# One core: y and the next chunk's scores in one visit to the quarters of TensorE, and another order at the start

## The chip, the cores and the metric

The kernel runs on one core of a Trainium2 chip, and on nothing else: there is no second core to wait for. The metric is the device time of one execution in microseconds (us), and for several runs its median. A core has five engines that run their own instruction streams and wait for each other by semaphores: PE (TensorE, the matmuls), DVE (VectorE), ACT (ScalarE), POOL (GpSimd) and SP (SyncE, which here only starts DMAs). ACT can start DMAs too.

## The reference, cut to what matters

```python
# gla: batch 4, 8 heads, 768 positions, head size 48
for t in range(S):
    state = alpha[:, :, t, :, None] * state + einsum('bhd,bhe->bhde', k[:, :, t], v[:, :, t])
    y[:, :, t] = einsum('bhd,bhde->bhe', q[:, :, t], state)
# bridge: (B, H, S, D) -> (B*S, H*D), so x is 3072 x 384
h = x @ w_in          # 384 x 2048
g = h - tanh(h)
out = g @ w_out       # 2048 x 384
```

Inputs and output are float32 here but for the weights, which come in 64-bit form and are brought to float32 on the chip.

## The kernel before, in words

Units. The 3072 rows are cut into 12 units of 256 positions (`NU`), and each unit into two chunks of 128 (`CU`). Three units make one batch element. For each unit there is a recurrent part, `gla`, and a feed-forward part, `moe`. In what follows "u.c" is chunk c of unit u, and "u:s" is step s of unit u's feed-forward part, of which there are eight (`FS`).

The recurrent part. The decays are transposed (`aT`), two scans on DVE make running products backwards and forwards (`U`, L711, and `W`, L730), and k and q are scaled by them (`kU`, `qW`). Then TensorE works per chunk in two small pieces. `scores` (L782 to L812) multiplies k by q within half chunks and makes the updates of the state. `y` (`halves_products`, L864 to L890) multiplies q with the state and the masked scores with v. From unit 1 on both use the array as four quarters of 64 x 64: 32 matmuls each, which the trace holds as 64 records, since each of them is recorded twice. Between them DVE masks the scores (`masked`), adds up `mid` and `state`, and decays the state (`decay`). After y, ACT copies the features to `xT` (`features`, task "x") and DVE adds the rest (`rest`); SP then moves a few rows (`moves`). `back` and `natural` transpose k for a unit and copy it. Unit 0 is done in another way (`direct`), with full masks and full-width scores.

The feed-forward part. Step u:s has a first product on TensorE (`first`, L1075: 6 matmuls of 256 columns, 12 records), a square and a quadratic on ACT (`u`, `z`), a cube on DVE (`w`, which reads h in PSUM), the shrunk value `g`, from unit 2 on three sums `e`, and a second product (`second`, L1117: 7 matmuls of 192 columns and 14 records, in units 0 and 1 four of 384). The weights of units 0 and 1 arrive in 16 pieces that SP fetches (`load_weight`, L39; eight DMAs for a piece of w_in), ACT reads (L86, L87) and DVE converts (L89, L90).

PSUM. Its pools are `ps_sc` (one tile of two banks, "sc"), `ps_h` (two tiles of one bank, "h": the results of first products) and `ps_o` (one bank each for "o0" to "o3": the results of second products). In the kernel before, y, the scores and `back` of units 2 to 11 all use the two banks of "sc", one after another.

The order. Nothing is scheduled at run time. Every task is added to `Planner` with an engine, a length in us, a rank and the tasks that it follows. `order` (L387) lays the tasks out eight times, with priorities from the round before (from the fifth on with random changes), and keeps the layout that ends first; each engine gets its instructions in that order. A task that follows another one is held back by that one's latency `lat`, also where both are on one engine. `filler` (L1204 to L1210) puts dummy matmuls ("spin") where the plan leaves TensorE idle before y 0.0. The task `see` loads the word `ok`, which says whether the fast path was valid, into all engines; the last unit's `store` comes after it.

In the middle of the run TensorE goes first product, scores, second product, first product, y, second product for a chunk, then some pairs of first and second product without a visit, then the next chunk; once a unit `back` comes in between.

Of the kernel before, what the change touches and what calls it, by code (L numbers as in the profile page):

```python
# [38 lines left out]
def load_weight(nc, pool, rows, **kw):  # L39

    raw = pool.tile([P, WN], I64 if rows[0][2].dtype != FP32 else FP32, name="raw", **kw)
    for at, js, src in rows:
        nc.sync.dma_start(out=raw[at].rearrange("p (j n) -> p j n", n=src.shape[-1])[:, js], in_=src)
    return raw
# [277 lines left out]
class Planner:  # L322
# [64 lines left out]
    def order(self):  # L387
# [3 lines left out]
        for i, t in enumerate(self.tasks):  # L391
            edges = {names[a]: self.tasks[names[a]][6] for a in t[4]}
            if t[7]:
                edges.setdefault(names[t[7]], 0.0 if self.tasks[names[t[7]]][1] == t[1] else 0.25)
            for j, lat in edges.items():
                before[i].append((j, lat))
                after[j].append((i, lat))
# [17 lines left out]
        for x in plan:  # L415
            name, e, length = self.tasks[x[3]][:3]
            if e == engine and until:
                filled += [(free, -1, do, None)] * int(max(0.0, x[0] - free) / us)
# [6 lines left out]
def fast(tc, q, k, v, alpha, moe_w_in, moe_w_out, out, w_in, w_out, ident, ok, pad_rows):  # L425
# [17 lines left out]
    with ExitStack() as ctx:  # L443
# [90 lines left out]

        plan = Planner()
# [15 lines left out]
        def fetch(what, s):  # L551
            raw_of[what, s] = load_weight(nc, raw_pool, weight_parts(moe_w_in, moe_w_out, pad_rows, what, s), bufs=4)
# [10 lines left out]
        for n, (what, s) in enumerate(pieces):  # L563
            rank = RANK[what] + 2 * s
            held = pieces[n - 4] if n >= 4 else None
            add(f"fetch {what}{s}", "SP", 5.7 if n < 2 else 4.3 if what == "in" else 2.0, rank - 30, [held and f"read {held[0]}{held[1]}"],
# [36 lines left out]
        def gla(u, rank):  # L603
# [8 lines left out]
            parts = [(x, slice(c * NP, (c + 1) * NP), slice(c, c + 1)) for c, x in enumerate("ab")] if parted else [("", slice(0, N), slice(0, CU))]  # L612
# [3 lines left out]
            def go(name, engine, us, k, after, do, of=u, **kw):  # L616
                add(f"{name} {of}", engine, us, rank + k,
                    [a if a[-1] in "0123456789" else f"{a} {of}" for a in after if a], do, **kw)

            prev = f" {u - 1}" if u > 0 else None  # L620
            for what, name in enumerate(("aT", "kT", "qT", "v")):
# [5 lines left out]
                   lambda what=what: load(u, what), lat=2.9 if u == 0 else 3.6 if u < PLAIN else 4.5)  # L627

            def widen(what):
                for hh in range(2):  # L630
                    t, r0 = raws[what], HP * hh
                    to, of = t[r0 + 32:r0 + HP, :, :, 0:D - 32], t[r0:r0 + 32, :, :, 32:D]
                    A.copy(to, of)  # L633

            def flip(what, make):
                t = make()
                for g in range(NP):
                    to = t[:, g].rearrange("p c (i r) -> p r c i", r=R)
                    V.transpose(to, raws[what][:, g, :, 0:32])  # L639
# [42 lines left out]
            for n, ab in enumerate("ab"):  # L682
# [3 lines left out]
                if by_matmul(u, 1):  # L686
                    go(f"turn kT{ab}", "PE", 0.92, 1 + n * 0.1,
                       ["load kT"] + [later and x for x in ("x 0.0", "y 0.1", "state 0.1")], lambda n=n: turn(1, n))
                    for x, _, cs in parts:
                        go(f"kU{ab}{x}", "DVE", 0.33 if x else 0.6, 3, [f"turn kT{ab}", f"U{x}", n and f"kUa{x}", later and "back 0.1", later and by_matmul(u, 2) and "turn qTb"],  # L690
                           lambda n=n, cs=cs: times(1, "U", n, cs))
                if by_matmul(u, 2):
                    go(f"turn qT{ab}", "PE", 0.92, 2 + n * 0.1,
                       ["load qT", later and f"aT{ab}" if by_matmul(u, 0) else "masked 0.0"], lambda n=n: turn(2, n))
                    for x, _, cs in parts:
                        go(f"qW{ab}{x}", "DVE", 0.33 if x else 0.6, 5, [f"turn qT{ab}", f"W{x}", n and f"qWa{x}", later and "y 0.1", later and by_matmul(u, 1) and "turn kTb"],
                           lambda n=n, cs=cs: times(2, "W", n, cs))
            for what, (name, k_) in enumerate((("aT", 0), ("kT", 2), ("qT", 4))):
                if by_matmul(u, what):
                    continue  # L700
                go(f"wide {name}", "ACT", 1.3, k_ - 0.5, [f"load {name}"], lambda what=what: widen(what))
                go(name, "DVE", 1.9, k_, [f"wide {name}"] + ([f"y {u - 2}.{CU - 1}"] if u > 1 else []),
                   lambda what=what: flip(what, makes[what]))
# [43 lines left out]
            for x, ns, _ in parts:  # L747
                go(f"U{x}", "DVE", 1.13 if x else 2.2, 1, (["aTa", "aTb"] if by_matmul(u, 0) else ["aT"])
                   + (kU(u - 1) + [f"sizeU{prev}", f"least{prev}"] if prev else []), lambda ns=ns: scan_U(ns))
                go(f"ends{x}", "DVE", 0.3, 3, [f"U{x}"], lambda ns=ns: ends(ns))  # L750
                go(f"W{x}", "DVE", 1.13 if x else 2.2, 3, [f"ends{x}"] + (qW(u - 1) + [f"sizeW{prev}"] if prev else []),
                   lambda ns=ns: scan_W(ns))
            whole = [x for x, _, _ in parts]
            go("least", "DVE", 0.07, 7, [f"U{x}" for x in whole], shortest)
            if not by_matmul(u, 1):
                go("kU", "DVE", 1.12, 3, ["kT", "U"], lambda: scale("kT", "U"))
            if not by_matmul(u, 2):
                go("qW", "DVE", 1.12, 5, ["qT", "W"], lambda: scale("qT", "W"))
# [11 lines left out]
            def chunk(c):  # L770
# [11 lines left out]
                def scores():  # L782
                    if c == 0:

                        xT[u] = two.tile([P, NP, TU], FP32, name="xT")
                    if u == 0 and c == 1:
                        sc = m["sc", c] = [ps_h.tile([P, 2, TU], FP32, name="h").rearrange(
                            "p a t -> p (a t)").rearrange("p (g t) -> p g t", t=P) for _ in range(2)]
# [25 lines left out]
                def masked():  # L814
                    sc = m["sc", c]
                    if direct:
                        m["pm", c] = [two.tile([P, NP, P], FP32, name=f"pm{r}", tag=tag) for r, tag in enumerate("zw")]
                        for r, to in enumerate(m["pm", c]):
                            V.tensor_mul(to, sc[r] if c else sc[:, r], mask.unsqueeze(1).to_broadcast([P, NP, P]))
# [14 lines left out]

                def products():

                    if n == 0:
# [26 lines left out]
                def halves_products():  # L864
# [4 lines left out]
                    m["y", c] = banks((2, 3))  # L869
# [22 lines left out]
                def rest():  # L892

                    for hh in range(2):
                        rows = quads[hh]
                        if u >= PLAIN:
# [10 lines left out]
                def features():  # L907
# [5 lines left out]
                    if u >= PLAIN:  # L913
# [46 lines left out]
                else:  # L960

                    held = [f"masked {past}"] if u == 1 and c == 0 else [f"masked {past}", f"mid {past}", f"state {past}"] if u == 1 else [
                        f"x {past}", f"rest {past}"] if c else []
                    go_c("scores", "PE", 1.27, 7, kU(u, c) + qW(u, c) + [f"natural {u}", f"load v {u}"] + held, scores)
# [357 lines left out]
```

## Time and profile before

| what | value |
|---|---|
| median of 3 runs (lowest, highest) | 576.52 us (575.82, 578.79) |
| the profiled execution's own time | 578.48 us |
| its span, from the first to the last instruction | 576.7 us |
| mean clock granted to TensorE | 0.992 |
| DMA moved | 50.84 MB |

The profile is of one execution, slower than the median by 2.0 us. Sums made from the trace belong to its own time. Its columns and views are explained where they are shown. What matters in reading it: the page gives busy shares over the whole span; the chain of work that ended last says on which engine a saved microsecond counts; the timeline gives the start of each group of instructions, and differences of starts are firmer than the lengths of matmuls, whose ends are modelled. These are the costliest groups of the page on TensorE, with the count and the mean length in nanoseconds:

```profile
L1080 PE MATMUL h<-xT,w_in 128*128 128x256 f32 x1152 | 265.1, 380 | 0.6 <-DVE w_in L90 0.6
...
L1146 PE MATMUL o<-b,e 128*128 128x192 f32 x480 | 90.9, 326 | 0.0
```

The last columns are the idle time of the engine just before the group and what ended it.

### The profile page before, as it was taken

The page shows a single profiled execution, that of the slowest core. Times are in us where ns is not written, and L with a number is a line of the kernel's source. Part 1 is how long each engine was busy: PE and PEld are TensorE (multiplying, and loading weights), DVE is VectorE, ACT ScalarE, POOL GpSimd, SP SyncE. Part 2 cuts the span into 40 slices and gives each one's busy share as a digit, 9 for nine tenths or more (in the row PEclk, how much of TensorE's full clock was granted, in tenths as well). Part 3 has the DMA queues.
Part 4 walks back from the last instruction along what each step waited for, and adds up shares of the span by engine and source line. Part 5 has one row for each costly group of instructions (what it writes and reads, how often), then busy time and mean ns, then how long its engine had stood idle before and what let it go on. Part 6 is the DMA issues. An engine that isn't in the chain of part 4 may idle for free.

```text
span 576.7 us, 13746 instructions
## 1 busy us (share of the span) xinstructions
PE 565.9 (98%) x5583; PEld 500.1 (87%) x5583; DVE 450.8 (78%) x886; ACT 323.2 (56%) x559; POOL 4.8 (1%) x22
## 2 busy tenths in 40 slices
PE   8899999999999999999999999999999999999995
PEld 8787777778989999998999999898998999899995
DVE  5889879999999995895895896896797645554643
ACT  2589885747777686577485365364443433333530
POOL 3000000000000000000000000000000000000000
PEclk9799999999999999999999999999999999999999
DMA  8988781235674762562640320310200000000001
GB/s 181 211 220 243 233 182 56 85 70 137 113 155 120 121 161 84 118 158 71 185 116 1 85 61 3 75 51 22 53 12 1 30 7 3 28 8 0 28 1 35
DMA packets 60713, 50.84 MB, mean 88 GB/s; under 512 B 35776, under 2 KB 50400, under 8 KB 60640
## 3 DMA queue, kind: packets, MB, share of 16 engines
q1 hardware_dynamic: 57728, 48.88, 34.7%
q10 hardware_dynamic: 2912, 0.98, 0.8%
q8 instruction: 46, 0.75, 0.6%
q14 instruction: 27, 0.22, 0.1%
HBM read 44.04 MB, written 4.72 MB: 85 GB/s over the span
## 4 chain that ended last, share of the span: by engine, by line
PE 96%; DVE 2%; issue 1%; POOL 0%; ACT 0%; DVEq 0%; POOLq 0%
PE h L1080 43%; PE o L1146 32%; PE o L1125 7%; PE sc L805 2%; PE sc L878 2%; PE sc L888 2%; PE sc L811 2%; PE sc L991 1%; PE spin L1208 1%; PE turned L663 1%; DVE W L730 0%; PE sc L795 0%; PE h L795 0%; DVE w_in L90 0%; PE y L853 0%
## 5 line engine op out<-in xcount | busy, mean ns | idle before, releaser
L1080 PE MATMUL h<-xT,w_in 128*128 128x256 f32 x1152 | 265.1, 380 | 0.6 <-DVE w_in L90 0.6
L1080 PEld LDWEIGHTS h<-xT,w_in 128*128 128x128 f32 x1152 | 215.4, 190 | 28.0 <-DVE w_in L90 0.7
L1089 ACT ACTIVATE u<-h 128x512 f32<-128x512 f32 x96 | 57.0, 594 | 180.7 <-PE h L1080 180.2
L1097 DVE TENSOR_TENSOR w<-h,u 128x512 f32<-128x512 f32 x96 | 65.8, 686 | 79.1 <-ACT u L1089 78.7
L1146 PE MATMUL o<-b,e 128*128 128x192 f32 x480 | 90.9, 326 | 0.0
L1146 PE MATMUL o<-w_out,e 128*128 128x192 f32 x320 | 81.5, 337 | 0.0
L1146 PEld LDWEIGHTS o<-b,e 128*128 128x128 f32 x480 | 80.2, 190 | 0.0
L1101 DVE SCALAR_TENSOR_TENSOR g<-z,w 128x512 f32<-128x512 f32 x96 | 65.3, 682 | 4.1 <-PE o L1125 1.3
L1146 PE MATMUL o<-b,g 128*128 128x192 f32 x320 | 65.1, 326 | 0.0
L1093 ACT ACTIVATE z<-u 128x512 f32<-128x512 f32 x96 | 60.4, 629 | 2.6
L1146 PEld LDWEIGHTS o<-w_out,e 128*128 128x128 f32 x320 | 55.7, 189 | 4.4
L1146 PEld LDWEIGHTS o<-b,g 128*128 128x128 f32 x320 | 54.2, 190 | 0.0
L1107 ACT ACTIVATE big<-u 128x1024 f32<-128x1024 f32 x48 | 50.4, 1049 | 0.0
L1125 PE MATMUL o<-w_out,g 128*128 128x384 f32 x128 | 44.0, 488 | 0.0
L1125 PEld LDWEIGHTS o<-w_out,g 128*128 128x128 f32 x128 | 24.1, 190 | 13.7
L1113 DVE TENSOR_TENSOR e<-g 128x256 f32<-128x256 f32 x80 | 33.4, 418 | 1.8
L1114 DVE TENSOR_TENSOR e<-g 128x256 f32<-128x256 f32 x80 | 33.3, 416 | 0.0
L639 DVE STREAM_TRANSPOSE aT<-ar 128x256 f32<-128x256 f32 x44 | 28.4, 645 | 2.8 <-ACT ar L633 1.7
L730 DVE TENSOR_TENSOR_SCAN W<-aT,before 128x1032 f32<-128x1032 f32 (+1 forms) x13 | 27.7, 2132 | 0.0
L711 DVE TENSOR_TENSOR_SCAN U<-aT,after 128x1032 f32<-128x1032 f32 (+1 forms) x13 | 27.6, 2129 | 0.1
L1115 DVE TENSOR_TENSOR e<-g 128x128 f32<-128x128 f32 x80 | 22.6, 283 | 0.0
L639 DVE STREAM_TRANSPOSE qT<-qr 128x256 f32<-128x256 f32 x40 | 20.5, 629 | 0.0
(141 smaller groups left out, 560.3 us busy)
## 6 DMA issues: line engine op xcount, KB each, us to landing
raw<-in_moe_w_out_dram SPq DMA_DIRECT2D x16, 768.0 KB, 4.8
raw<-in_moe_w_in_dram SPq DMA_DIRECT2D x80, 96.0 KB, 4.0
raw<-in_moe_w_in_dram SPq DMA_DIRECT2D x16, 288.0 KB, 5.1
vt<-in_v_dram SPq DMA_DIRECT2D x23, 192.0 KB, 4.1
ar<-in_alpha_dram SPq DMA_DIRECT2D x44, 96.0 KB, 2.5
kr<-in_k_dram SPq DMA_DIRECT2D x40, 96.0 KB, 3.3
qr<-in_q_dram SPq DMA_DIRECT2D x40, 96.0 KB, 2.3
out_dram<-cross SPq DMA_DIRECT2D x19, 96.0 KB, 1.7
```

The source lines that it names most:

```text
L639: V.transpose(to, raws[what][:, g, :, 0:32])
L730: V.tensor_tensor_scan(out=m["W"][:, ns].rearrange("p n t -> p (n t)"), data0=aT[:, a:z], data1=before[:, a:z], initial=0.0, op0=ALU.mult, ...
L1080: T.matmul(h[:, a, :], lhsT=w_in[:, j, f * P:(f + 1) * P], rhs=xT[u][:, j, :], start=(j == 0), stop=(j == KT - 1))
L1089: A.activation(m["u", s], m["h", s], AF.Square, scale=W_SCALE ** -1.5)
L1093: A.activation(m["z", s], m["u", s], AF.Square, bias=QB, scale=QA * W_SCALE)
L1097: V.tensor_mul(m["w", s], m["h", s], m["u", s])
L1101: V.scalar_tensor_tensor(out=g.rearrange("p a c t -> p (a c t)"), in0=m["z", s], scalar=QK, in1=m["w", s], op0=ALU.add, op1=ALU.mult)
L1107: A.activation(big, m["us", s // 2].rearrange("p s t -> p (s t)"), AF.Relu, bias=-U_FAST, scale=W_SCALE, accum_out=over[:, n:n + 1])
L1113: V.tensor_add(e[:, 0:2, :], g[:, 0], g[:, 1])
L1114: V.tensor_sub(e[:, 2:4, :], g[:, :, 1, :], g[:, :, 0, :])
L1125: T.matmul(m["o"][c], lhsT=g[:, a, c, :], rhs=w_out[:, f, :], start=(f == 0), stop=(f == FT - 1))
L1146: T.matmul(o[n][:, i], lhsT=g_, rhs=w_, start=(s_ == 0 and (n, i) in ((0, 0), (1, 0), (2, 1), (3, 0))), stop=(s_ == FS - 1), skip_group_ch ...
```

## The change

- **Joint visits.** From unit 3 on (`JOINT`), y of a chunk is followed on TensorE at once by the scores of the next chunk. The place is fixed: `behind` names the step of the unit before after whose first product the pair comes (0 for chunk 0 and 4 for chunk 1, in unit 3 the steps 2 and 5), and `row`, a chain of tasks written out by hand, fixes the order of first products, second products and pairs from unit 2 on. After a pair come the second product of the step before and then two first products in a row.
- **y in other banks.** For these units y takes both tiles of "h" in place of the tile "sc". So y follows the cube of the last first product, and the next first product follows x and rest. As the tiles are now two, x is two copies and rest four adds, as in units 0 to 2 before.
- **Unit 0's scores** take banks of "o" and "h" in place of "sc", and `xT` is made with y.
- **Smaller tasks.** `widen` and `flip` are cut into pieces, and the scans U and W of every unit into two halves, each with its own `ends`.
- **The planner.** A task that follows one on the same engine (but for SP) is no longer held back by a latency. The rounds, the seed and the random changes are not touched by the diff. The dummy matmuls are counted with 0.24 us in place of 0.35 and in another formula. Lengths of tasks are changed, and ACT begins at 5.4.
- **The first piece of w_in** is fetched by ACT and SP in turn, four DMAs each; ACT's come after its copy of aT.

The built order of the changed kernel also differs where no line asks for it: the verdict's transpose comes after the last second product on TensorE, and unit 0's four products of k come before the first scan W on DVE.

```diff
-def load_weight(nc, pool, rows, **kw):
+def load_weight(nc, pool, rows, queues=None, **kw):
-    for at, js, src in rows:
-        nc.sync.dma_start(out=raw[at]..., in_=src)
+    for n, (at, js, src) in enumerate(rows):
+        (queues[n % len(queues)] if queues else nc.sync).dma_start(out=raw[at]..., in_=src)
...
-            edges = {names[a]: self.tasks[names[a]][6] for a in t[4]}
+            edges = {names[a]: 0.0 if self.tasks[names[a]][1] == t[1] != "SP" else self.tasks[names[a]][6] for a in t[4]}
...
-                filled += [(free, -1, do, None)] * int(max(0.0, x[0] - free) / us)
+                gap = x[0] - free
+                filled += [(free, -1, do, None)] * int(gap / (1.5 * us) if free == self.begin.get(engine) else (gap + 0.3) / us if gap > 0.2 else 0)
...
+        JOINT = PLAIN + 1
+        def behind(u, c):
+            return ((5 if c else 2) if u == JOINT else 4 * c) if u >= JOINT else None
+        def following(u, c):
+            after = (u, c + 1) if c + 1 < CU else (u + 1, 0)
+            return after if u >= JOINT and after[0] < NU else None
...
+                    if u == 0:
+                        sc = m["sc", c] = [(ps_h if c else ps_o).tile([P, NP, P], FP32, name="scores", tag="h" if c else f"o{r}")
+                                           for r in range(2)]
...
-                    m["y", c] = banks((2, 3))
+                    m["y", c] = banks((2, 3)) if u < JOINT else [ps_h.tile([P, NP, P], FP32, name="y", tag="h") for _ in range(2)]
...
+                near = [f"cube {u - 1}:{behind(u, c)}"] if behind(u, c) is not None else []
+                go_c("y", "PE", 1.19 if following(u, c) else 1.29, 9, near + ["masked", "mid", ...], halves_products)
...
+        joint = {(u - 1) * FS + behind(u, c): [f"y {u}.{c}"] + [f"scores {v}.{c_}" for v, c_ in [following(u, c) or (NU, 0)] if v < NU] for u in range(JOINT, NU) for c in range(CU)}
+        for at in range(PLAIN * FS, NU * FS + 2):
+            first, second, third = (f"{n // FS}:{n % FS}" for n in (at, at - 2, at - 1))
+            row += [f"first {first}"] * (at < NU * FS)
+            if at in joint:
+                row += [f"second {second}"] + joint[at] + [f"second {third}"]
+            elif at - 1 not in joint:
+                row.append(f"second {second}")
...
                 add(f"first {me}", "PE", 2.59, r, [...]
+                    + [f"{what} {u + 1}.{c}" for c in range(CU) if u + 1 < NU and behind(u + 1, c) == s - 1 for what in ("x", "rest")], first)
...
-        plan.filler = "PE", "y 0.0", 0.35, spin
-        plan.begin.update(SP=0.8, PE=1.5, ACT=3.0, DVE=4.8)
+        plan.filler = "PE", "y 0.0", 0.24, spin
+        plan.begin.update(SP=0.8, PE=1.5, ACT=5.4, DVE=4.8)
```

## The prediction

> **What bounds the kernel now.** I read the page's busy table, its forty slices and the chain that ended last first: is one engine the bound from end to end, and where is it not?
>
> ```profile
> span 576.7 us, 13746 instructions
> ...
> PE 565.9 (98%) x5583; PEld 500.1 (87%) x5583; DVE 450.8 (78%) x886; ACT 323.2 (56%) x559; POOL 4.8 (1%) x22
> ...
> PEclk9799999999999999999999999999999999999999
> ...
> PE 96%; DVE 2%; issue 1%; POOL 0%; ACT 0%; DVEq 0%; POOLq 0%
> ```
>
> TensorE carries 96% of the chain. So a microsecond taken out of TensorE's own sequence is worth a microsecond, and DVE and ACT count only where they make it wait. Two places are not covered by that: the second slice, where the clock digit is 7, and the last slice, where TensorE's digit is 5. I then opened the timeline of TensorE in the steady part, at one first product with a second product behind it, and at the two kinds of visit to the quarters.
>
> ```profile
> 208.60 2.77 PE L1080 MATMUL h<-xT,w_in 128*128 128x256 f32 x12
> 211.30 0.69 PE L805 MATMUL sc<-qT,kT 48*64 48x64 f32 x32
> 211.81 0.62 PE L811 MATMUL sc<-vt,kn 64*64 64x48 f32 x32
> 212.36 0.59 PE L1146 MATMUL o<-w_out,e 128*128 128x192 f32 x2
> ...
> 214.74 2.75 PE L1080 MATMUL h<-xT,w_in 128*128 128x256 f32 x12
> 217.42 0.34 PE L878 MATMUL sc<-qT,state 48*64 48x64 f32 x8
> 217.59 0.30 PE L878 MATMUL sc<-qT,mid 48*64 48x64 f32 x8
> ...
> 217.94 0.65 PE L888 MATMUL sc<-pm,vt 64*64 64x64 f32 x32
> 218.51 0.59 PE L1146 MATMUL o<-w_out,e 128*128 128x192 f32 x2
> ...
> 220.90 2.75 PE L1080 MATMUL h<-xT,w_in 128*128 128x256 f32 x12
> 223.49 0.49 PE L1146 MATMUL o<-w_out,e 128*128 128x192 f32 x2
> ...
> 225.76 2.75 PE L1080 MATMUL h<-xT,w_in 128*128 128x256 f32 x12
> ```
>
> Columns are start, length, engine, line. The reader is to take differences of starts. A first and a second product without a visit take 225.76 - 220.90 = 4.86 us. With the y visit the same pair takes 220.90 - 214.74 = 6.16, with the scores visit 214.74 - 208.60 = 6.14. A visit costs 1.30 or 1.28 us.
>
> How much of it is work? Inside y the third and fourth groups of 8 records start 0.12 apart (the chain gives the last 31 records 0.47), so about 14.7 ns a record: 64 records are 0.94. The scores have 32 such records (0.47) and 32 of L811 at 0.44 in the chain: 0.91. So 1.30 - 0.94 = 0.36 and 1.28 - 0.91 = 0.37 us of each visit is going in and coming out: about 0.15 before and in the first group (217.42 comes 2.68 after the first product's start where 2.59 is usual, and the first group takes 0.17, not 0.12), the rest in the second product after it (2.39 rather than 2.27, and a late start).
>
> The start and the end, by windows and the timeline:
>
> ```profile
> 15.00:20.00 5.00, 3.00 (x24) 2.58 (x23) 2.88 (x9) 2.45 (x5) 0.00 (x0) 0.75 0.77 197
> 20.00:25.00 5.00, 5.00 (x54) 4.12 (x54) 4.75 (x9) 2.82 (x5) 0.00 (x0) 0.57 1.17 256
> ```
>
> After the window and its length stand busy time and count of PE, PEld, DVE, ACT, POOL, then the clock. TensorE idles 2 us before 17.64 (the waits put it on DVE's qT) and then runs at half clock until about 24.3: the same 16 score records take 2.08 us here.
>
> ```profile
> 565.25 0.27 PE L1239 MATMUL sc<-ident,fine 128*1 128x128 f32 x1
> ...
> 565.57 0.28 DVE L1243 TENSOR_REDUCE ok<-sc 1x1 int32<-1x128 f32 x1 [0.21 <-PE sc L1239]
> ...
> 568.17 0.49 ACT L1184 ACTIVATE p<-o 128x384 f32<-128x384 f32 x1 [4.96 <-PE o L1146]
> ```
>
> The verdict's transpose stands in front of TensorE's last 28 records; the queues load ok at 565.9 (0.47 us), and p starts before TensorE has ended.
>
> **What the Trainium skill says.** TensorEngine Tiling (Array Packing), Tiling Modes: changing the tiling mode drains the engine, moving to another tile in the same mode doesn't. The trace agrees: 0.36 us at the borders of a visit, none seen between L805 and L811 or L878 and L888. TensorE: Matmul & The Clock Gate, Part 1: the clock is either half or full, decided by how busy TensorE was in a window of about 3.4 us. The trace agrees in kind: half clock for 6.8 us after an idle stretch. DMA: Bandwidth & Descriptors, Issuing engines are not separate DMA queues: a second issuing engine saves issue time only. The trace has SP issuing the first piece of w_in from 4.60 to 11.47 us, with 232 GB/s moved in the window from 5 to 10 us.
>
> **The change, part by part**, from the trace's durations and from the order in which both built kernels hold their instructions.
>
> Joint visits. The built order has 44 separate visits before and 26 after: 17 from unit 3 on hold y and the next scores back to back, and one early (unit 1). A joint visit pays one border instead of two. From the trace 0.36 us each; the bound below is 0.2, if the first scores matmul starts its own weight loads late, and above 0.37. I take 0.33: 17 x 0.33 = 5.6 us. The early one I count at nothing, since DVE sets the pace there.
>
> What the joint visit makes wait. y now writes the two h banks, so it waits for the cube of the first product just before. In the trace that first product's end is followed by u at 217.53 and w from 218.16 to 218.85, 1.43 us after 217.42; y comes one second product later, 2.27. Slack 0.8, and the cover is that second product. Behind y on TensorE stand the scores, a second product and the next first product, which needs both banks back: x (two copies of 0.36 in place of one of 0.57) and rest (four adds of 0.28 in place of two of 0.42), about 2.1 us with hand-overs after y; the scores and the second product cover 1.2 + 2.3 = 3.5. DVE's order puts two to three 0.6 us flips ahead of rest, still inside. Cost nothing; without cover up to 1.2 us a visit, a halved scan or a kT multiply in front of the cube. The two first products in a row after each joint visit cost nothing (5.38 for 24 records at 133.52 in the chain, which holds one exit of 0.20).
>
> DVE and ACT get more to do: 0.15 us of rest and 0.06 of x per chunk, and per unit about 0.4 us of DVE for halved scans with their own ends. Over nine units some 7 us of DVE, which idles 126. It is full from 80 to 185 us (some 103 of 105), but there it works ahead. Nothing, at most 2.
>
> The start. The changed order has TensorE spin before update, scores and y, so the idle 2 us is filled; the chunk-0 qT products come before the second W, so scores 0.0 can start about 15.6 and not 17.64. From DVE's row lengths: kT x4 to 13.1, ends and W to 14.5, ends and two qT to 15.5, W to 16.6, two qT to 17.3, state to 17.6, masks to 18.9 and 20.2. The direct products then run at full clock from about 19 to 24, against 28.5 before. That is 4.4 us at this point. It is not all kept, for DVE then sets the pace: from 20.2 two conversions (1.5 each) to 23.2, four flips and the state to 26.0, U to 28.3, two ends and W to 31.2, two kT and two qT to 33.8, so scores 1.0 about 34.8 (41.11 before, after another first product); the third conversion and two cubes to 36.6, so the third first product near 36.1; cubes, masks and the fourth conversion to 39.4, where the fourth first product starts. From there two first products (2.59), two visits of y, one of scores without its borders (0.92) and two second products of unit 0 (2.58) end at about 53.3. Before, the same work had ended at 57.1 by the chain: 3.6 ahead. From that I take 0.6 for the new order on ACT: it issues half of the first piece after its aT copy, where four DMAs cost SP 3.4 us, and reads that piece before it copies state, for which DVE's decay and the masks behind it wait. SP is 3.4 us sooner at the second piece. So 3.0, with 0.5 (the clock halves again) and 4.5 as bounds.
>
> The end. The built order now holds all 21 last second-product matmuls and the transpose of the verdict after them. Before, p started at 568.17 while TensorE ran to about 570.1 (28 records x 0.1625 us from 565.53): 1.9 before its end. Now ok is ready only after it: transpose to load's end is 566.40 - 565.42 = 1.0 us, so p starts 1.0 after TensorE's end. The end moves by 2.9 us. The rest of it (p, four DVE instructions, the stores) is as before.
>
> Sum: -5.6 - 3.0 + 2.9 = -5.7 us. The profiled execution took 578.48 us, its span 576.7; it would become 572.8, its span 571.0. Its own time stands 2.0 above the median, 576.52, from which the same step gives 570.8.
>
> **Rivals.** (1) The start is not kept: spins too few or in the wrong window, or ACT's issuing delays state. For it: ACT's queue is in the way of state, and DMA was already busy. Against: TensorE's fillers now cover nearly every gap. Gain 0.5 instead of 3.0: 573.3.
> (2) The change doesn't do what it says: y to scores costs a border too. Against it is the seamless step between L805 and L811; for it, that no trace here shows y next to scores. Joint 0: 576.4.
> (3) Slower: y held by the cube. If DVE starts a 1.2 us instruction just before u is done, the cube ends 0.55 after its slack at each of 17 visits and the next first product slips along: 17 x 0.55 = 9.4, so 570.8 + 9.4 = 580.2. It eats the gain from 0.34 us a visit and decides against the change from 0.5. For it: DVE's busy digits and its fixed order. Against: the built order splits the flips and scans that were 2.3 us long.
>
> **How the numbers follow.** The likeliest case, 0.58: 570.8, by itself 568.5 to 573.5. Rival 1: 0.17. Rival 2: 0.10. Rival 3: 0.10. Full value on both gains (17 x 0.37 + 4.5 - 2.9 = 7.9, so 568.6): 0.05. About 0.5%, 2.9 us, can be told from no change. Faster by more: 0.55 + 0.10 + 0.05 = 0.70; slower: 0.10; the rest, 0.20, within. Range: 567.5, below the full value by some scatter, to 576.0, which takes in rival 1 and most of rival 2.
>
> **What would show it.** Right: visits of 128 records about 2.2 us long, and 9.3 to 9.4 from the start of the first product before them to the next (4.86 + 2.2 + 2.27); TensorE waiting on DVE's w for under 0.1 each; a clock digit of 9 in the second slice; first h near 24 to 25 us; the verdict's transpose last on TensorE, p a microsecond later. Wrong: TensorE waits for cube or rest with ten or more counts, a clock digit still at 7, or TensorE's busy time not smaller by about 5.

## The result, and the profile after

The changed kernel takes 594.23 us (median of 4 runs, 592.64 to 596.01) beside 576.17 for the kernel before on the same chip: the ratio is 1.030, with an interval of 1.026 to 1.035. The forecast was 570.8, faster. The profiled execution took 592.64 us, its span is 590.9, 14.2 more than before. That is less than the 18.1 between the medians, because this execution was the fastest of its kernel, 1.6 below its median, and that of the kernel before was 2.3 above its own (576.17); sums from the traces add up to the 14.2. First the page of the changed kernel: busy table, granted clock, chain of work that ended last.

```profile
span 590.9 us, 13863 instructions
...
PE 563.2 (95%) x5593; PEld 501.6 (85%) x5593; DVE 472.9 (80%) x966; ACT 326.4 (55%) x577; POOL 4.8 (1%) x22
...
PEclk9899999999999999999999999999999999999998
...
PE 59%; DVE 29%; issue 5%; DMA 3%; ACT 2%; ACTq 0%; DVEq 0%; SPq 0%
```

TensorE is 2.7 us less busy than before (565.9), yet the span is longer, and its share of the chain fell from 96% to 59%: DVE now sets the pace for 29% of the run. DVE's busy time rose by 22 us. The view of waits says where TensorE stood still (engine, line, who was waited for, then us in total, times, longest):

```profile
PE y L902 <- DVE w L1137: 8.7, 8, 1.6
...
PE h L1120 <- DVE xT L929: 1.7, 5, 0.5
...
PE y L949 <- ACT state L977: 1.5, 1, 1.5
PE sc L902 <- DVE mid L969: 1.2, 1, 1.2
```

Eight times y waited for the cube `w`. Before, no such line existed. Two joint visits show the difference, first a clean one (the visit at step 4:4, timeline of TensorE: start, length, engine, line).

```profile
243.60 2.75 PE L1120 MATMUL h<-xT,w_in 128*128 128x256 f32 x12
...
249.34 0.34 PE L902 MATMUL y<-qT,state 48*64 48x64 f32 x8
...
250.31 0.66 PE L822 MATMUL sc<-qT,kT 48*64 48x64 f32 x32
250.78 0.65 PE L828 MATMUL sc<-vt,kn 64*48 64x48 f32 x32
251.35 0.59 PE L1186 MATMUL o<-w_out,e 128*128 128x192 f32 x2
...
253.73 0.59 PE L1120 MATMUL h<-xT,w_in 128*128 128x256 f32 x2
```

From first product to first product it takes 253.73 - 243.60 = 10.13, of which 0.77 are `back` (and 0.03 its border); y follows the second product without a gap, the scores follow y without a border, the visit lasts 2.0. Now the visit half a unit earlier, at step 4:0:

```profile
220.50 2.75 PE L1120 MATMUL h<-xT,w_in 128*128 128x256 f32 x12
...
225.46 0.33 PE L902 MATMUL y<-qT,state 48*64 48x64 f32 x4
226.97 0.27 PE L902 MATMUL y<-qT,state 48*64 48x64 f32 x2 [1.18 <-DVE w L1137]
...
228.90 0.59 PE L1186 MATMUL o<-w_out,e 128*128 128x192 f32 x2
...
231.28 1.03 PE L1120 MATMUL h<-xT,w_in 128*128 128x256 f32 x4
```

10.78 without `back`, where a clean visit takes 9.33 (the one after 10:0 does): 1.45 lost, all of it between y's first records and the second product behind the scores. The bracket names the releaser. DVE in the same microseconds:

```profile
221.79 0.67 DVE L1137 TENSOR_TENSOR w<-h,u 128x512 f32<-128x512 f32 x1
222.56 0.69 DVE L1141 SCALAR_TENSOR_TENSOR g<-z,w 128x512 f32<-128x512 f32 x1
...
224.17 1.22 DVE L754 TENSOR_TENSOR kT<-kT,U 128x1024 f32<-128x1024 f32 x1
225.30 1.10 DVE L658 STREAM_TRANSPOSE qT<-qr 128x256 f32<-128x256 f32 x2
226.25 0.68 DVE L1137 TENSOR_TENSOR w<-h,u 128x512 f32<-128x512 f32 x1
...
228.63 1.11 DVE L658 STREAM_TRANSPOSE qT<-qr 128x256 f32<-128x256 f32 x2
...
229.60 0.98 DVE L929 TENSOR_TENSOR xT<-y,xT 48x128 f32<-48x128 f32 x4
```

The first product ended at about 223.1. A kT multiply and two flips of the next unit stand in front of its cube, which starts at 226.25; y needs both h banks and goes on only when it ends. Two more flips stand in front of `rest` at 229.60. At this visit that costs nothing more: the first product at 231.28 comes 2.38 after the second product before it, as in the clean visit (253.73 - 251.35). After 3:0, 5:0, 6:0, 7:0 and 9:0 the first product does wait for `rest` (the five times in the view above) and comes 0.4 to 0.6 later. There is no bracket on these DVE rows: DVE had no idle time here that the view marks, it worked off its fixed order.

So I went through the starts of all first products, and took from each distance the lengths that undisturbed work has in these traces (first product 2.59, second 2.275, in units 0 and 1 2.58; `back` 0.77, y 0.94, scores 0.91, border 0.36). What is left is waiting. Against the kernel before:

| from | us |
|---|---|
| first product 0:0 starts at 28.73, not 31.07 | -2.3 |
| transposes for unit 0 and 1 that now come after it | +2.6 |
| borders of visits, 26 in place of 44, 0.36 each | -6.5 |
| waits in the eight joint visits for chunk 0 (after 2:2, and after u:0 of units 3 to 9; 1.4 to 2.3 each) | +15.3 |
| other waits (up to step 0:3 1.3, before 1:7 1.4, rest 0.3) | +3.0 |
| the end: a second product of 2.28 that stood behind the last first product now stands before it, and the stretch after that first product is still 18.4 (18.6) | +2.1 |
| sum | +14.2 |

Of the 15.3, some 11.2 lie where y waits for its cube and 3.0 in front of the two first products that follow; 1.1 lie at the visit after 2:2, where the second product in front of y waits for ACT. The joint visits for chunk 1, and the last one for chunk 0 after 10:0, beside which no unit is prepared, wait for nothing.

### The profile page after: what moved, and what is told of

Its sections match the earlier page's. It is cut to its first block, busy times and chain, and to the rows that moved or that the text cites. A ratio compares the mean times of both kernels' runs of the same rounds, so it can differ in the third digit from the quotient of the medians.

```text
span 590.9 us, 13863 instructions
## 1 busy us (share of the span) xinstructions
PE 563.2 (95%) x5593; PEld 501.6 (85%) x5593; DVE 472.9 (80%) x966; ACT 326.4 (55%) x577; POOL 4.8 (1%) x22
## 4 chain that ended last, share of the span: by engine, by line
PE 59%; DVE 29%; issue 5%; DMA 3%; ACT 2%; ACTq 0%; DVEq 0%; SPq 0%
PE h L1120 29%; PE o L1186 18%; PE o L1165 5%; DVE g L1141 3%; DVE W L749 3%; DVE w L1137 3%; DVE kT L658 2%; DVE qT L658 2%; DVE aT L658 2%; DVE U L730 2%; DVE e L1154 2%; DVE xT L929 2%; PE y L902 2%; DVE kT L754 2%; DMA raw<-in_moe_w_in_dram 1%
## 5 line engine op out<-in xcount | busy, mean ns | idle before, releaser
L1186 PE MATMUL o<-w_out,e 128*128 128x192 f32 x320 | 80.1, 333 | 0.9 <-ACT same L1220 0.9
L749 DVE TENSOR_TENSOR_SCAN W<-aT,before 128x516 f32<-128x516 f32 x24 | 29.6, 1232 | 0.7
L730 DVE TENSOR_TENSOR_SCAN U<-aT,after 128x516 f32<-128x516 f32 x24 | 29.0, 1224 | 0.3
L944 ACT COPY xT<-y 112x256 f32<-112x256 f32 (+2 forms) x42 | 13.4, 371 | 25.3 <-PE y L912 24.1
L929 DVE TENSOR_TENSOR xT<-y,xT 48x128 f32<-48x128 f32 x80 | 19.5, 283 | 7.3 <-ACT xT L944 6.9
```

The costliest lines, as they stand in the source:

```text
L730: V.tensor_tensor_scan(out=m["U"][:, ns].rearrange("p n t -> p (n t)")[:, ::-1], data0=aT[:, z:a:-1], data1=after[:, a:z][:, ::-1], initia ...
L749: V.tensor_tensor_scan(out=m["W"][:, ns].rearrange("p n t -> p (n t)"), data0=aT[:, a:z], data1=before[:, a:z], initial=0.0, op0=ALU.mult, ...
L1186: T.matmul(o[n][:, i], lhsT=g_, rhs=w_, start=(s_ == 0 and (n, i) in ((0, 0), (1, 0), (2, 1), (3, 0))), stop=(s_ == FS - 1), skip_group_ch ...
```

## The experiments

Times are medians; the chip's kernel before stood at 575.8 to 578.4 in these sessions. I give the ratio to it with its interval, and from the trace the period of a unit: the mean distance of the first products of step 5 (7 without joint visits) from unit 4 to 9. It is 44.81 us for the kernel before and 45.99 for the changed one. The last column adds up, over seven units, what the distance from first product u:0 to u:2 has beyond 11.94, the sum of the undisturbed lengths above. Period and waits are of one profiled execution each. e1 to e4 ran where the kernel before stood at 578.4 and the changed kernel where it stood at 576.2, so that differences of their medians hold to about 1 us.

| run | us | ratio (interval) | period | waits of the visits after u:0, units 3 to 9 |
|---|---|---|---|---|
| changed kernel | 594.23 | 1.030 (1.026 to 1.035) | 45.99 | 13.0 |
| e1_light_dve | 585.94 | 1.015 (1.010 to 1.019) | 45.21 | 7.5 |
| e2_sp_only | 590.55 | 1.022 (1.018 to 1.027) | 45.99 | 13.0 |
| e3_no_joint | 585.66 | 1.015 (1.010 to 1.020) | 45.06 | 4.6 (y alone) |
| e4_lat_back | 583.43 | 1.009 (1.006 to 1.012) | 45.50 | 9.2 |
| f1_sp_lat | 581.35 | 1.010 (1.007 to 1.014) | 45.49 | 9.1 |
| f2_no_joint_lat | 576.08 | 1.000 (0.998 to 1.002) | 44.81 | none |
| f3_before_zero | 587.66 | 1.019 (1.016 to 1.022) | 44.81 | 0.1 |
| f4_true_lengths | 574.44 | 0.997 (0.996 to 0.998) | 44.32 | 1.8 |
| g1_true_late | 573.59 | 0.995 (0.994 to 0.997) | 44.24 | 0.8 |
| g2_cube_wide | 575.53 | 0.999 (0.997 to 1.001) | 44.22 | 1.8 |
| g3_true_only | 576.93 | 1.001 (1.000 to 1.003) | 44.56 | 2.4 |
| g4_no_joint_true | 575.93 | 1.000 (0.998 to 1.002) | 44.81 | none |
| h1_other_plan | 597.14 | 1.034 (1.029 to 1.038) | 45.93 | 11.8 |
| h2_shorter | 594.77 | 1.031 (1.027 to 1.035) | 45.40 | 9.6 |
| h3_flips_only | 579.22 | 1.003 (1.002 to 1.005) | 44.79 | 5.1 |
| h4_true_sp | 575.53 | 0.998 (0.997 to 1.000) | 44.55 | 2.4 |

**Is it DVE's queue?** The first run makes DVE's work lighter and leaves every other instruction in its place. It leaves out the four flips of aT of each unit from 3 to 11, 36 instructions (the expectation names units 3 to 9).

```diff
-                V.transpose(m["to", what][:, g]..., raws[what][:, g, :, 0:32])
+                if what > 0 or u < JOINT:
+                    V.transpose(m["to", what][:, g]..., raws[what][:, g, :, 0:32])
```

> Left out: DVE's four flips of aT in units 3 to 9 (four times 0.63 us a unit); the decays are then those of the unit two before, all else and the order of every other instruction are the changed kernel's. Theory (the cube in front of the c = 0 joint visit stands behind the unit's preparation on DVE, which is full there): the 1.4 to 2.3 us that each of these visits loses shrink by most of 2.5 us, so 8 to 14 us less than the changed kernel, 580 to 586, and the wait of y on DVE's w falls from 8.7 us to under 3. Rival (y in the product's banks must wait, whatever DVE has to do): within 2 us of the changed kernel's 594.

8.3 us less in the median, at the lower end, and 7.6 in the profiled span. The wait of y on w fell to less than a third:

```profile
PE y L903 <- DVE w L1138: 2.6, 6, 0.7
```

So the cube stands behind the preparation, and y waits for that and not by its nature. More than half of all the waiting at these visits stayed (7.5 of 13.0): at step 5:0 TensorE still lost 0.36 before y and 0.45 before the next first product, which waits for `rest` behind a flip and the qT multiply. 1.6 us of the gain lie before the first product, where the edit changes nothing (why, the next experiment shows). So some 6 us are DVE's.

**Start.** One word of the fetch is put back; the plan is the same, instruction by instruction.

```diff
-                                          queues=[A, nc.sync] if (what, s) == pieces[0] else None, bufs=4)
+                                          queues=None, bufs=4)
```

> The changed kernel with the first piece of w_in issued by SP alone, as before the change; the plan is untouched. Theory (four issues on ACT of 1.3 us each hold up gaps, the read and the copy of state, and with them TensorE): the early part gets back 1 to 4 us, so 590 to 593, and the copy of state starts about 3 us sooner than 18.86. Rival (the start is set by the landing of the data, which both queues together do not speed up or slow down): within 0.7 us of 594.

3.7 us less in the median and 2.3 in the profiled span. The first product 0:0 comes 3.8 sooner (24.95 in place of 28.73), of which 1.0 is lost again by step 1:3; the period is untouched. The timeline of the start in the changed kernel, then its windows (busy time of PE, PEld, DVE, ACT, POOL, then clock, DMA share, GB/s):

```profile
7.82 5.36 ACTq L43 DMA_DIRECT2D raw<-in_moe_w_in_dram  x4
13.28 0.27 ACT L847 COPY v_gap<-vt 128x96 f32<-128x96 f32 x1 [5.94 <-DMA raw<-in_moe_w_in_dram]
17.02 1.06 ACT L86 ACTIVATE more<-raw 128x768 int16<-128x768 uint32 x1 [2.00 <-DMA raw<-in_moe_w_in_dram]
18.86 0.29 ACT L977 COPY state<-y 112x192 f32<-112x192 f32 x1
```

```profile
15.00:20.00 5.00, 3.42 (x43) 3.06 (x44) 2.15 (x5) 3.00 (x5) 0.00 (x0) 0.94 0.67 175
20.00:25.00 5.00, 4.90 (x47) 4.09 (x47) 2.87 (x7) 2.79 (x7) 0.00 (x0) 0.72 0.85 217
```

And with SP alone:

```profile
9.75 0.27 ACT L847 COPY v_gap<-vt 128x96 f32<-128x96 f32 x1 [1.88 <-DMA vt<-in_v_dram]
14.79 1.08 ACT L86 ACTIVATE more<-raw 128x768 int16<-128x768 uint32 x1 [1.26 <-DMA raw<-in_moe_w_in_dram]
16.66 0.29 ACT L977 COPY state<-y 112x192 f32<-112x192 f32 x1
```

```profile
15.00:20.00 5.00, 4.54 (x51) 3.82 (x52) 4.38 (x10) 4.95 (x10) 0.00 (x0) 1.00 0.78 211
20.00:25.00 5.00, 4.97 (x89) 3.90 (x88) 4.59 (x10) 2.96 (x6) 0.00 (x0) 1.00 0.70 195
```

Four issues hold ACT for 5.36 us, 1.3 each, and they do not bring the piece sooner: the read starts at 17.02 and not at 14.79. The copy of state behind it is 2.2 later (expected: 3), TensorE idles 1.5 us for it, and its clock falls to 0.72 where it stays full with SP alone. The two losses can be told apart by e1, whose start is the changed kernel's, instruction for instruction. Its read starts at 17.00, as late as here, but its clock is 1.00 from 15 to 30 us, and its first product comes at 27.12. So the issues themselves cost 27.12 - 24.95 = 2.2 us before the first product, and the halved clock 1.6 more. The clock is not halved in every execution, but seldom spared: of the eight variants with both queues (the changed kernel, e1, e3, e4, g3, h1, h2, h3) seven profiles show it below 1 between 15 and 25 us, of the eight with SP alone (e2, f1, f2, f4, g1, g2, g4, h4) none.

**Joint visits or not.** JOINT is set to the number of units, so that y goes to the quarters and is visited apart, with the conditions of the kernel before where they differ.

```diff
-        JOINT = PLAIN + 1
+        JOINT = NU
...
-                        if u == PLAIN:
+                        if PLAIN <= u < JOINT:
```

> The changed kernel without joint visits: from unit 3 on y and scores are visited apart and y goes to the quarters again, as before; start, plan, filler and the end stay changed. Theory (the joint visits save 6.1 us of borders and lose 15.3 in waits behind DVE): about 9 less than the changed kernel, 585, with y's wait on w gone; at the least 581 if the early waits shrink too. Rival (the loss comes from the new plan and the start, and the joint visits do help): about 600.

585.66, as expected, but not wholly for the reason: without joint visits y alone now waits too, for DVE's `state`, five times and 5.4 us. The kernel before has no such wait. Something in the plan itself is worse, with joint visits or without.

**The planner's 0.** The change lets a task follow another on its own engine at once; before, the planner kept 0.3 us between them.

```diff
-            edges = {names[a]: 0.0 if self.tasks[names[a]][1] == t[1] != "SP" else self.tasks[names[a]][6] for a in t[4]}
+            edges = {names[a]: self.tasks[names[a]][6] for a in t[4]}
```

> The changed kernel with the planner's old cost for two tasks in a row on one engine that depend on each other (0.3 us in place of 0), so that the plan sets other work between w, g and e again. Theory (such pairs cost 0.12 to 0.18 us more each on DVE and lengthen the preparation where DVE is full): 2 to 8 us less than the changed kernel, 586 to 592, with w to g 0.60 apart again. Rival (these pairs do not matter, DVE's sum of work does): within 1.5 us of 594.

10.8 us less, more than expected. DVE's busy time falls from 472.9 to 457.7 with the same 966 instructions. In the rows above w to g takes 0.77 (221.79 to 222.56); in this run, where something else follows w, that starts after some 0.6, before w's 0.67 are over. g follows w directly 54 times of 96, in the changed kernel 89 times, before 26 times. Of the 8.3 us in the profiled span, 4.4 lie between first product 0:0 and step 3:1, only 2.4 between 3:1 and 10:7, where most of the joint visits stand, and 1.5 at the end. The same line was then put into the kernel before, and both single edits into the changed one:

> Both single edits at once: the first piece of w_in by SP alone, and the planner's old cost between dependent tasks of one engine. They cost in different places (start, and DVE's queue in the steady part), so the gains add: 583.4 - 3.7 = 579.7. Rival (the old cost already mends the start, or ACT's issues matter only with the new order): 582 to 584.

> As the run with both edits, but without joint visits and without the row that fixes TensorE's order: y and scores apart, y in the quarters. Theory (even with the old cost the c = 0 joint visits lose about 9.7 us over eight visits against 6.1 saved): about 3.6 less, 576, level with the kernel before. Rival (with the old cost the joint visits help): 582 to 586.

> The kernel before with one line of the change: the planner takes 0 in place of 0.3 us between two dependent tasks of one engine. Theory (w and g then stand back to back, each such pair costs DVE 0.12 to 0.18 us more, and visits come late): DVE's busy time up by 8 to 15 us and the time up by 2 to 7 us, 579 to 584. Rival (harmless without joint visits): within 1.5 us of before.

f1 falls short of its forecast by 1.6 in the median, but in the profiled spans the gain adds as expected (582.6 to 578.7, first product 0:0 at 24.30 in place of 28.70). f2 is level with the kernel before, so with the 0.3 back joint visits still lose 5.3 us: 45.49 a unit against 44.81. It also says that what else the change brings (smaller tasks, unit 0's other banks, the other fillers) gains nothing in the median. f3 loses 11.9 us, more than expected, and not where I expected it: its period is still 44.81, and all of it lies before step 4:1. The clock page of that run has a 6 in the second slice, where the kernel before has a 7:

```profile
PEclk9699999999999998999999999999999999999998
```

Its first product starts at 32.66 (31.07), waits up to 0:3 are 2.9 longer, and single ones of 1.2, 2.1 and 3.4 stand at 2:1, 2:6 and 4:0 (1.7 of the last is a second product at half clock). So this plan loses at the start and at single spots. Whether the 0 does that or the other order that any changed number brings is not shown: h1 below moves the first product by 7 us with the 0 left as it is. In the steady part of the kernel before, where no visit stands close behind a cube, the 0 is harmless.

**The planner's lengths.** From the trace, the four flips of aT take 2.53 us where the plan has 1.9, the two small instructions of `ends` 0.42 where it has 0.3, w and g in a row 1.5 where it has 1.2. In the four steps in front of the visit after u:0, which hold a unit's preparation, that is 0.63 + 2 x 0.12 + 4 x 0.3 = 2.1 us that DVE needs and the plan does not know of, beside 15.3 / 8 = 1.9 us of waiting.

```diff
-                pieces_of(name, "DVE", 1.9, k_, ...
+                pieces_of(name, "DVE", 2.05 if what else 2.53, k_, ...
-                go(f"ends{x}", "DVE", 0.3, 3, ...
+                go(f"ends{x}", "DVE", 0.4, 3, ...
-                add(f"cube {me}", "DVE", 0.6, ...
+                add(f"cube {me}", "DVE", 0.66, ...
...
```

> As the run with both edits, with the lengths of DVE's tasks in the planner set to what the trace shows (flips of aT 2.53 for four in place of 1.9, kT and qT 2.05, ends 0.4, scans 1.16, multiplies 1.15, mid and state 0.38, w 0.66, sums 0.9). Theory (the planner puts the preparation in front of the cube because it believes it shorter than it is): most of the 9.7 us left at the c = 0 visits goes, 572 to 576, below the kernel before. Rival (the lengths hardly change the order, or DVE has no room in that stretch): within 2 us of the run with both edits.

> As the run with the true lengths, but these hold from unit 3 on only, so that the early units are planned as in the run with both edits, where step 1:3 was reached 2.3 us sooner. Theory (the lengths matter where joint visits stand, the loss of that run before 1:3 is chance of the plan): 571 to 573.5. Rival (the plan is one piece, and another random spot gets worse): 574 to 578.

> As the run with the true lengths, with w at 0.8 us in the planner in place of 0.66, so that DVE is left more room in front of y. Theory (what is left of the waits of y, about 2 us over eight visits, comes from w planned too tight): 572 to 574. Rival (the room only pushes other work of DVE later): 574 to 578.

> The changed kernel with the true lengths alone; the 0 between dependent tasks of one engine and both queues stay. Theory (both the 0 and the short lengths make DVE's plan tighter than the chip; either alone leaves part of the 15.3 us): 582 to 589, with y still waiting some 3 to 5 us on w. Rival A (the lengths are the whole cause): 577 to 580. Rival B (the 0 is): 592 or more.

> As the run with the true lengths, without joint visits and without the fixed row: y in the quarters, apart from the scores. It shows what joint visits are worth once DVE's plan is right. Theory (17 borders of 0.36 less some 3 us of waits that are left): 3 us more than the run with the true lengths, 577 to 578, or level with the run without joint visits, 576. Rival (the lengths alone make the gain): 574.5 or less.

f4: 574.44, the waits of the visits fall from 9.1 to 1.8 and it is below the kernel before. g1 is the fastest kernel of the study, 573.59, 0.1 above its forecast; it reaches step 1:3 at 88.9 as f1 does, and f4 at 91.2. g2 has the shortest period but lost 4.2 us before step 0:7, where a second product waited for a converted weight (2.3 in the view of waits) and then ran at a lower clock, and 1.7 more at the second first product behind the visit after 3:0; its time is in its rival's range. g3 contradicts what I expected: the lengths alone, with the 0 and both queues left in, take 17.3 us off. Its rival A is right, to 0.1. Its busy table and one visit:

```profile
PE 559.7 (97%) x5591; PEld 501.1 (87%) x5591; DVE 470.2 (82%) x966; ACT 326.2 (57%) x577; POOL 4.8 (1%) x22
```

```profile
212.20 2.75 PE L1120 MATMUL h<-xT,w_in 128*128 128x256 f32 x12
...
217.16 0.34 PE L902 MATMUL y<-qT,state 48*64 48x64 f32 x8
...
221.53 0.81 PE L1120 MATMUL h<-xT,w_in 128*128 128x256 f32 x3
```

```profile
216.03 0.67 DVE L1137 TENSOR_TENSOR w<-h,u 128x512 f32<-128x512 f32 x1
...
218.41 1.22 DVE L754 TENSOR_TENSOR kT<-kT,U 128x1024 f32<-128x1024 f32 x1
219.54 0.64 DVE L658 STREAM_TRANSPOSE qT<-qr 128x256 f32<-128x256 f32 x1
220.03 0.97 DVE L929 TENSOR_TENSOR xT<-y,xT 48x128 f32<-48x128 f32 x4
```

DVE is as busy as in the changed kernel (470 us), yet the visit at 4:0 takes 9.33. The kT multiply stands behind the cube now, not in front of it, and `rest` follows one flip. After 5:0, 7:0, 8:0 and 9:0 the multiply still stands in front, but without flips, and y goes on only 0.2 to 0.7 late. It is the order that cost, not the amount of work. g4 prices the visits: 44.81 a unit without them, 44.32 in f4 with them. Over nine units that is 4.4 us; the medians differ by 1.5 (574.44 and 575.93), as the two plans differ elsewhere too (f4's first product comes 1.3 later).

**Lengths, or only another draw?** Any number changed makes the planner choose another order, so that g3 might have been luck. Four more runs; the first changes a latency of unit 0's loads (2.5 to 2.7), the second the lengths the wrong way (1.9 to 1.6, 0.3 to 0.25), the third the first line of the diff above alone, the fourth joins true lengths and SP alone.

> A control: the changed kernel with a planner's number that has nothing to do with DVE (the latency of unit 0's loads, 2.7 in place of 2.5 us), which makes it choose another order. Theory (too short lengths of DVE's preparation are what puts it in front of y): the period of a unit stays near 46.0 us and the whole near the changed kernel's, 590 to 597, apart from what the start does. Rival (the changed kernel's order was an unlucky draw, and any other would do): period 44.5 or less, under 584.

> The changed kernel with DVE's lengths moved the wrong way: flips of a unit's aT, kT and qT 1.6 in place of 1.9 each, ends 0.25 in place of 0.3. Theory: the preparation is planned tighter still, the period stays at 46.0 or grows, 592 to 600. Rival (any other order is better): under 586.

> The changed kernel with one length mended, that of the flips: aT 2.53 for four in place of 1.9, kT and qT 2.05. They are 1.03 of the some 1.9 us by which a unit's preparation was planned too short (the rest: two ends 0.2, scans and multiplies 0.2, mid and state 0.24 a chunk). Theory: a good half of the stall goes, period 44.8 to 45.3, 580 to 586. Rival (the tasks next to y count, w and mid, not the flips): period 45.7 or more, 590 or more.

> True lengths with the first piece of w_in by SP alone; the 0 between dependent tasks stays. The two gains lie in different places and add as in the other pair: 576.9 - 3.7 = 573.2, period 44.5 as in the run with the true lengths alone. Rival (issuing by ACT costs nothing here, as the read of that piece is planned elsewhere): 576 to 577.5.

Another order with the same lengths is no better in the steady part, 45.93; its 597.14 us also hold a first product that comes 7.0 later (35.74). Lengths moved the wrong way keep the loss: 594.77. Against what I expected the period is shorter (45.40), while the visit after 2:2 alone waits 4.8 us. So the loss doesn't simply grow with the error of the lengths. The flips alone take 15.0 of the 17.3 us (579.22, period 44.79), a little more than expected. h4 gained 1.4 in the median and 3.0 in the profiled span of the 3.7 expected, so that the issues seem to cost less with this order; the interval ends at the kernel before (0.9997).

Over all plans with joint visits: those with the old lengths (the changed kernel, e4, f1, h1, h2) have periods from 45.4 to 46.0, those with the flips mended (f4, g1, g2, g3, h3, h4) from 44.2 to 44.8. With six plans on one side and five on the other, the steady loss comes with the old lengths and is not one unlucky order's. What the 0 costs beside mended lengths can't be told: h4 has it and f4 doesn't, and their intervals overlap. What stays open: I had taken some lengths from busy times rather than from distances of starts (kT and qT flips 2.05 where starts say 1.9, state 0.38 where they say 0.27), so that the plan got some room beside the truth, and the runs don't tell how much of the 17.3 us is due to either.

## Why the prediction was wrong, point by point

- **Joint visits, 17 x 0.33 = 5.6.** Right. Clean visits have no border inside; where the plan leaves DVE room, a unit takes 44.22 to 44.32 in place of 44.81, 0.25 to 0.3 a visit with the waits that are left, and the borders alone gave 6.5 over 18 visits (the 18th is the early one, counted at nothing).
- **"What the joint visit makes wait ... Cost nothing."** This is the step that failed. I took slack 0.8 from one cube in the trace of before, in front of which DVE had been idle, as the bracket says:

```profile
218.16 0.69 DVE L1097 TENSOR_TENSOR w<-h,u 128x512 f32<-128x512 f32 x1 [1.39 <-ACT u L1089]
```

It was not the rule there either. Of the 80 cubes of that trace from step 2:0 on, 31 end more than 2.4 us after their first product (its length taken as 2.59), later than y would have come, and cost nothing as no visit waited for them. I named the cover and its end, "a halved scan or a kT multiply in front of the cube" at 1.2 us a visit, and then did not look in the built order for it: it has just that multiply and two or three flips there after 4:0 to 9:0, and halved scans after 2:2 and 3:0. At eight of 17 visits this cost 1.9 us each, 15.3 in all, y's wait for the cube and the waits around it together.
- **"DVE ... idles 126 ... it works ahead. Nothing, at most 2."** It failed with it. DVE's idle time lies elsewhere: from 205.7 to the visit shown it works without a gap that the view marks. It was 22 us busier and not 7; 15 of that go in e4, where fewer dependent instructions stand back to back, and these I had left out.
- **Rival 3, 580.2 with a chance of 0.10,** was the right mechanism with the wrong size: 0.55 at all 17 visits, where it is 1.9 at eight, those with a preparation in front.
- **The start, 3.0 gained.** By step 0:3 1.6 us were lost. The first product came 2.3 sooner but left 2.6 of transposes behind it, and the waits up to 0:3 are 1.3 longer. ACT's issues, which I counted at 0.6, cost 2.2 before the first product, and 3.8 with the clock that was halved again (e2 and e1), as rival 1 had it. From the Trainium skill I had the two sides: that a second issuing engine saves issue time only (DMA: Bandwidth & Descriptors, Issuing engines are not separate DMA queues), which the read at 17.02 bears out, and that the clock is half or full by how busy TensorE was in a window of about 3.4 us (TensorE: Matmul & The Clock Gate, Part 1), which the 0.72 after two stretches of 1.5 us idle bears out in kind, while e1, with stretches of 1.07 and 1.26, keeps it full; neither was weighed against ACT's fixed order.
- **Signs.** Of the three signs of being wrong two came: 13 waits for cube or `rest`, and TensorE's busy time smaller by 2.7 and not 5. The clock digit was 8.
- **The end, 2.9.** Nearly right: the verdict's transpose came last on TensorE at 581.89 and p 1.2 after it, and the whole end costs 2.1.

The saving of the joint visits was thus as forecast, and the loss came from what the plan put beside them. With DVE's lengths, the 0.3 and SP alone mended (g1), the median is 573.59 beside 575.85 for the kernel before in the same session: 2.3 us less, where 5.7 had been forecast for the change as it was. (The profiled spans differ by more, 570.5 and 576.7, since g1's profile is of its fastest execution.)

## What to carry to other kernels

When a change ties an instruction closer behind another engine's result, look up in the built order what stands in front of that result at every place where it happens, not at one place in the old trace. A written plan is only as good as its lengths: before the plan is tightened, set its lengths by a trace (distances of starts would be the better source, which no run here tests by itself), since a plan that has slack hides wrong lengths (the kernel before ran its steady part at 44.81 with them) and a tight one doesn't. An average of idle time says nothing of the stretch in front of the wait. And an order that is sought anew after every edit needs controls with other orders: here one alone moved the start by 7 us.

## What the runs showed of the hardware that was not expected

- On DVE, g, which reads w, starts 0.79 after it back to back (the middle of 89 pairs in the changed kernel, 0.73 to 0.82; both 128 x 512 float32); an instruction that doesn't read w starts 0.58 to 0.61 after it, inside w's recorded 0.67. That it is the reading and not the kind of instruction, the same pair shows: where g reads an earlier w, once in the kernel before (95.71 to 96.30) and three times in f3, it too starts 0.60 after the w in front of it. The Trainium skill (VectorE: DVE Perf Modes, The DRAIN you can't avoid) says that an operation which isn't held starts before the pipe is empty, which the 0.60 bears out, and that in a row of copies a wait on the one before cost nothing more. Here it differs: a dependent pair takes about 0.19 us more, and with more such pairs in a row DVE is busy 472.9 us (changed kernel) instead of 457.7 (e4) at equal instruction counts.
- Four DMAs issued by ACT from 7.82 on, while SP issued too, took 1.34 us each; SP's twelve took 0.91 each, and sixteen by SP alone 0.72 each (11.58 us in e2). Both queues together did not land the piece sooner.
